# Two chained feed-forward nets after a retention layer: when the second net's weights are prepared, and which buffers their loads use

## The chip, the cores and the metric

The kernel runs on one core of a Trainium2 chip. The metric is the device time of one execution in microseconds (us). The core has five engines that work side by side, each through its own queue in the order of the program: TensorE (PE), VectorE (DVE), ScalarE (ACT), GpSimd (POOL), and SyncE (SP), which here only starts DMA transfers.

## What is computed

```python
def _moe_ref(x, w_in, w_out):
    h = x @ w_in
    g = np.where(h >= 1, h, np.where(h <= -1, 0.0, (h + 1) ** 2 / 4.0))
    return g @ w_out
def _moe2_ref(x, w1, w2, w3, w_out):
    a = x @ w1
    b = x @ w2
    h = a * b @ w3
    return h @ w_out
```

`x` are the 3072 tokens by 512 features that a retention layer (a decayed linear attention of 4 batches and 8 heads) gives. The first net has 2048 hidden features, the second 1024. The second net has nothing nonlinear behind its product `a * b`, so `w3 @ w_out` is computed once, and one product with it (`wc`) follows `a * b`.

## The kernel before, in words

Every fp32 operand is split into a rounded part and a rest (`split`, L96: a copy on ACT, then a subtraction on DVE), and three matmuls make one product (`mm3`, L100).

**First net.** The tokens are six tiles of 512, the hidden features 16 blocks of 128. A step `n` is one block of one tile (the loop at L774). On PE it is twelve matmuls of `emit_h(n + 1)` (the next step's first product) and twelve of `emit_y1(n)`. Between them stand, on ACT and DVE, the nonlinear function of the step to come (`emit_g1`, L456: `r`), its split (`emit_g2`, L466: `gh`, `gl`), and the split of a block of `w_out` (`emit_wo`, L476: `wo_s`). So `emit_y1` of the next step needs what ACT and DVE do behind `emit_h` of this one. `f = n - 80` counts the steps of the last tile, 0 to 15. The order on every queue is the order of the program; no scheduler changes it.

**Preparation in the last tile** (L840 to L852). `prepare_ab(j)` (L606) takes one block of `w1` and `w2` from DRAM (`fetch_ab`, two loads of 256 KB), makes four sums on DVE and seven splits on ACT and DVE, and writes the result back to DRAM with two transfers, `wab_d<-four` of 1 MB and `wab_d<-three` of 0.75 MB (L625). All eight preparations lie here, one in each odd step. Even steps load a block of the second `w_out` (`fetch(("wo2", j))`) and split the one before it (`load_wo2`, L552). All these loads go through `fetch` (L271), into one set of five buffers, and are issued on SP at L273, behind whatever SP has to issue before.

**The product of the last two weights** (L859 to L882). For `u` from 0 to 15, `emit_w3o(u)` (L563) is twelve matmuls with a block of `w3` and a block `wo2`; `load_w3(u + 1)` (two buffers) splits the next block, and the block after that is fetched. `evac_w3o` splits the four sums into `wc` at `u` = 7 and 15. In the same loop the first net's result for the first pair of tiles is read back (`fetch_y1`, four loads a half), added up (`add_y`, L641: four operations on DVE) and split (`split_y`, L654), seven splits a half, for the second net.

**Second net** (L885 on): `emit_ab(i, f, fill)` and `emit_out`; its weights come by `load_unit`, two loads of 1 MB and 0.75 MB. `c5` (L683) has one buffer of its own.

Of the kernel before, what the change touches and what calls it, by code (L numbers as in the profile page):

```python
# [9 lines left out]
F32 = mybir.dt.float32  # L10
# [6 lines left out]
P = 128  # L17
# [5 lines left out]
TT = 512  # L23
NTILE = NT // TT
NK = DM // P
NP = H // 2
NF1, NF2 = FF1 // P, FF2 // P
# [10 lines left out]
PLAIN = 11  # L38
SINGLE = 1
LATE = 5  # L40

# [5 lines left out]
def retention_then_two_ffns(  # L49
# [219 lines left out]
    arrived = {}  # L269

    def fetch(key, src):  # L271
        t = late.tile([P, 512], F32, tag="f", name="f32", bufs=5)
        nc.sync.dma_start(out=t, in_=src)  # L273
        arrived[key] = t

# [276 lines left out]
    def load_wo2(j):  # L552
        t = new_w("wo2")
        split(t[:, 0, :], t[:, 1, :], arrived.pop(("wo2", j)))
        wo2[j] = t
# [46 lines left out]
    def fetch_ab(f):  # L602
        for w in range(2):
            fetch(("wab", 2 * f + w), spill[("wab", 2 * f + w)])
# [31 lines left out]
    def fetch_y1(i, kb, which):  # L636

        for j in which:
            fetch(("y", i, kb, j), y1_d[2 * i + j % 2][kb + 2 * (j // 2)])
# [19 lines left out]
    def emit_ab(i, f, fill):  # L659
        w = units.pop(8 * i + f)  # L660
        bank = ps_h.tile([P, TT], F32, tag="h", name="bank_a")
        ps_p2 = ps_b.tile([P, TT], F32, tag="p2", name="bank_c")
        ps_p5 = ps_b.tile([P, TT], F32, tag="p5", name="bank_b")
        fill = list(fill)

        def product(name, ps, first):
            for kb in range(2):
                t, y = w[name], yops[(i, kb, name)]
                lh, ll, rh, rl = t[:, 0, kb, :], t[:, 1, kb, :], y[:, 0, :], y[:, 1, :]
                for k, (x, z) in enumerate(((lh, rh), (ll, rh), (lh, rl))):  # L670
                    nc.tensor.matmul(  # L671
                        out=ps, lhsT=x, rhs=z, start=first and kb + k == 0,
                        stop=kb == 1 and k == 2, skip_group_check=True,
                    )

        def between():
            if fill:
                emit_out(*fill.pop(0))

        c1 = work.tile([P, TT], F32, tag="r", name="c1")  # L680
        c2 = late.tile([P, TT], F32, tag="c2", name="c2", bufs=2)
        c3 = late.tile([P, TT], F32, tag="c3", name="c3", bufs=1)
        c5 = late.tile([P, TT], F32, tag="c5", name="c5", bufs=1)  # L683
        product("p1", bank, True)
        nc.scalar.copy(out=c1, in_=bank)
        product("p2", ps_p2, True)
        nc.vector.tensor_tensor(out=c1, in0=ps_p2, in1=c1, op=ALU.add)
        between()
        product("p6", bank, False)
        nc.scalar.copy(out=c2, in_=bank)  # L690
        product("p5", ps_p5, True)
        nc.scalar.copy(out=c5, in_=ps_p5)
        between()
        product("p7", bank, False)
        nc.scalar.copy(out=c3, in_=bank)
        product("p3", ps_p5, False)
        nc.vector.tensor_tensor(out=c2, in0=ps_p5, in1=c2, op=ALU.add)  # L697
        nc.vector.tensor_tensor(out=c3, in0=c3, in1=c5, op=ALU.add)
        nc.vector.tensor_tensor(out=c2, in0=c2, in1=c3, op=ALU.mult)
        between()  # L700
        product("p4", bank, False)
        nc.vector.tensor_tensor(out=c1, in0=bank, in1=c1, op=ALU.mult)
        between()
        ph = split_pool.tile([P, TT], F32R, tag="gh", name="ph")
        pl = split_pool.tile([P, TT], F32R, tag="gl", name="pl")
        split(ph, pl, c1)
        p0[f] = (ph, pl)
        ph = wpool.tile([P, TT], F32R, tag="wo", name="qh")
        pl = wpool.tile([P, TT], F32R, tag="wo", name="ql")
        split(ph, pl, c2)  # L710
        p1[f] = (ph, pl)
# [21 lines left out]
    with tc.manual_schedule():  # L733
# [40 lines left out]
        for n in range(-1, NA):  # L774
            last = n + 1 == NA
            if n < HALF - 1:
                mine = 1 if n % 2 else 2
            elif n < NF1 + 3:
                mine = 0
            elif n < NF1 + HALF - 2:  # L780
                mine = 1
            elif n < 2 * NF1 - 1:
                mine = (len(todo) - (NSTEP - 3 * TILE_PIECES) + 2 * NF1 - 2 - n) // (2 * NF1 - 1 - n)
            else:
                mine = 1 if (n + 1) % 4 < 3 else 0
            mine = [todo.popleft() for _ in range(mine) if todo]
            if n == PLAIN - 1:
                drain_conv()
                conversion.close()
                split_pool = splits.enter_context(tc.tile_pool(name="split_pool", bufs=2))  # L790
                cpool = conversion.enter_context(tc.tile_pool(name="cpool1", bufs=2))
                jobs.extend(later)
                load_job(jobs[0])
                load_job(jobs[1])
                for j in range(NF2):
                    jobs.append((w_out2[j], 512, ("wo2", j), done_spill(("wo2", j))))
                for j in range(NF2):
                    for i, w in enumerate((w1, w2)):
                        key = ("wab", 2 * j + i)
                        jobs.append((w[j], 512, key, done_spill(key)))  # L800
                for u in range(2 * NF2):
                    hf, j = divmod(u, NF2)
                    key = ("w3", u)
                    jobs.append((w3t[j][:, hf * 512:(hf + 1) * 512], 512, key, done_spill(key)))
            for i in range(2):
                if n == NF1 + (i + 1) * HALF - 4:
                    fetch_part(i)
            if n == NA - NF1:
                assert not todo
                drain_conv()  # L810
            f = n - (NA - NF1)
            if not last:
                emit_h(n + 1)
            if mine:
                piece_mm(mine[0])
                chunk_ahead(mine[0])
            if not last:
                emit_g1(n + 1)
            if mine:
                piece_ew(mine[0])  # L820
            if not last and f:
                emit_g2(n + 1)
            if n >= 0:
                emit_y1(n)
                evac_y1(n)
            if not f:

                conversion.close()
                splits.close()
                retention.close()  # L830
                split_pool = ctx.enter_context(tc.tile_pool(name="split_late", bufs=2))
                late = ctx.enter_context(tc.tile_pool(name="late", bufs=1))
                emit_g2(n + 1)
            if not last:
                emit_wo(n + 1)
            for a in mine[1:]:
                piece_mm(a)
                chunk_ahead(a)
                piece_ew(a)
            if f >= 0:  # L840
                j = f // 2
                if f % 2 == 0:
                    if j == 0:
                        fetch_ab(0)
                    else:
                        load_wo2(j - 1)
                    fetch(("wo2", j), spill[("wo2", j)])
                else:
                    prepare_ab(j)
                    if j + 1 < NF2:  # L850
                        fetch_ab(j + 1)
        load_wo2(NF2 - 1)  # L852
        pairs_psum.close()
        ps_b = ctx.enter_context(tc.tile_pool(name="ps_b", bufs=1, space=bass.MemoryType.PSUM))

        def y_of(i, kb):
            return [(i, kb, name) for name in ORDER]

        fetch(("w3", 0), spill[("w3", 0)])  # L859
        load_w3(0)  # L860
        fetch(("w3", 1), spill[("w3", 1)])
        fetch_y1(0, 0, range(4))
        for u in range(2 * NF2):
            load_w3(u + 1)
            if u + 2 < 2 * NF2:
                fetch(("w3", u + 2), spill[("w3", u + 2)])
            emit_w3o(u)
            hf, j = divmod(u, NF2)
            if j == NF2 - 1:
                evac_w3o(hf)  # L870
            if u == 0:
                add_y(0, 0)
            if u == NF2:
                add_y(0, 1)
            if u < NK + 3:
                split_y(*y_of(0, 0)[u])
                if u >= 3:
                    fetch_y1(0, 1, [u - 3])
            elif u > NF2:
                split_y(*y_of(0, 1)[u - NF2 - 1])  # L880
            if u in (2 * NF2 - 4, 2 * NF2 - 2):
                load_unit((u - 2 * NF2 + 4) // 2)  # L882


        for i in range(NTILE // 2):  # L885
            more = i + 1 < NTILE // 2
            ahead = y_of(i + 1, 0) + y_of(i + 1, 1)
            for f in range(NF2):
                emit_ab(i, f, out_blocks(f - 1) if 0 < f < NF2 - 1 else ())
                if 8 * i + f + 2 < 8 * (NTILE // 2):  # L890
# [95 lines left out]
```

## Time and profile before

| | us |
|---|---|
| median of three runs | 1108.55 (1107.0 to 1108.69) |
| the profiled execution's own time | 1108.74 |
| its span in the trace | 1106.9 |
| PE busy in the span | 1053.5 |
| DVE busy | 700.9 |
| ACT busy | 435.0 |

The rows of the profile have this form: start in us from the span's beginning, duration, engine, line and operation, output<-inputs by the program's names, tile sizes, count; in brackets the idle time of the engine before it and what ended it. `SPq` is SP's queue; an SP row is the issue of a transfer, not the transfer. The modelled durations of matmuls overlap, so a matmul's price is read from the distance between two starts. Busy engines say little by themselves: a stage is as long as the wait that ends last in it.

### The profile page before, as it was taken

The numbers are of one execution on the slowest core, as the hardware profiler recorded it, in microseconds if no ns is written. First come the engines' busy times: TensorE is split into PE (matmuls) and PEld (weight loads), VectorE is DVE, ScalarE is ACT, GpSimd is POOL, SyncE is SP. The second block draws the span as 40 slices with busy tenths as digits, with TensorE's granted clock in tenths as the row PEclk, the third lists the DMA queues.
The fourth block names the chain that finished last, engine by engine and source line by source line (L and its number), as shares of the span: only waits on it lengthen the run. The fifth ranks groups of instructions, "written<-read, shape, count | busy, mean of one in ns | idle before, by whom it ended". The sixth has DMA issues, their size and how long they took to land.

```text
span 1106.9 us, 14137 instructions
## 1 busy us (share of the span) xinstructions
PE 1053.5 (95%) x5444; PEld 832.1 (75%) x5444; DVE 700.9 (63%) x1130; ACT 435.0 (39%) x763; POOL 61.8 (6%) x51
## 2 busy tenths in 40 slices
PE   5789999899999999999999995899999999999998
PEld 4555578677777777777788784778888888888887
DVE  4698888688878878877835775553455344623341
ACT  1223355344444445444435664343233223412220
POOL 2212000011110100000000000000000000000000
PEclk9999999999999999999999997899999999999999
DMA  6545224345543444354302667554554355523412
GB/s 216 172 144 175 91 96 161 106 155 179 168 155 126 152 153 151 125 166 149 115 2 104 235 217 276 166 200 168 178 177 143 125 171 180 190 102 136 162 38 76
DMA packets 64116, 166.03 MB, mean 150 GB/s; under 512 B 7600, under 2 KB 15920, under 8 KB 59312
## 3 DMA queue, kind: packets, MB, share of 16 engines
q1 hardware_dynamic: 64048, 165.12, 44.0%
q8 instruction: 43, 0.70, 0.2%
q14 instruction: 25, 0.20, 0.1%
HBM read 125.24 MB, written 39.85 MB: 149 GB/s over the span
## 4 chain that ended last, share of the span: by engine, by line
PE 80%; DVE 8%; DMA 6%; ACT 3%; SPq 2%; issue 1%; POOL 0%; DVEq 0%; POOLq 0%; ACTq 0%
PE bank_a L671 12%; PE hps L102 7%; PE hps L103 7%; PE hps L101 7%; PE y1acc L101 7%; PE bank_b L671 6%; PE y1acc L102 6%; PE y1acc L103 6%; PE oacc L716 4%; PE oacc L718 4%; PE oacc L717 4%; DMA f<-sp_wab 3%; PE bank_c L671 3%; PE pa L370 3%; PE pa L346 2%; PE y1acc L511 1%
## 5 line engine op out<-in xcount | busy, mean ns | idle before, releaser
L101 PE MATMUL hps<-xh,win 128*128 128x512 f32 x384 | 155.6, 405 | 6.8 <-ACT win L97 5.5
L102 PE MATMUL hps<-xh,win 128*128 128x512 f32 x384 | 153.0, 398 | 0.7 <-DVE win L98 0.7
L103 PE MATMUL hps<-xl,win 128*128 128x512 f32 x384 | 152.0, 396 | 0.2 <-DVE xl L415 0.2
L101 PE MATMUL y1acc<-gh,wo_s 128*128 128x512 f32 x340 | 139.6, 411 | 6.6 <-ACT wo_s L97 6.6
L671 PE MATMUL bank_a<-yop,unit 128*128 128x512 f32 x576 | 145.7, 389 | 0.0
L459 ACT ACTIVATE r<-hps 128x512 f32<-128x512 f32 x96 | 57.3, 597 | 215.2 <-PE hps L103 215.2
L102 PE MATMUL y1acc<-gh,wo_s 128*128 128x512 f32 x340 | 135.6, 399 | 0.9 <-DVE wo_s L98 0.9
L103 PE MATMUL y1acc<-gl,wo_s 128*128 128x512 f32 x340 | 134.2, 395 | 0.0
L461 DVE SCALAR_TENSOR_TENSOR r<-hps,r 128x512 f32<-128x512 f32 x96 | 66.4, 691 | 99.4 <-ACT r L460 98.8
L671 PEld LDWEIGHTS bank_a<-yop,unit 128*128 128x128 f32 x576 | 108.0, 188 | 22.5
L697 DVE TENSOR_TENSOR c<-bank_b,c 128x512 f32<-128x512 f32 x24 | 16.6, 692 | 131.5 <-PE bank_b L671 131.5
L101 PEld LDWEIGHTS hps<-xh,win 128*128 128x128 f32 x384 | 73.3, 191 | 26.0 <-ACT win L97 6.2
L102 PEld LDWEIGHTS hps<-xh,win 128*128 128x128 f32 x384 | 73.3, 191 | 18.9 <-issue 1.7
L103 PEld LDWEIGHTS hps<-xl,win 128*128 128x128 f32 x384 | 73.4, 191 | 16.8 <-DVE xl L415 0.9
L101 PEld LDWEIGHTS y1acc<-gh,wo_s 128*128 128x128 f32 x340 | 64.3, 189 | 25.9 <-ACT wo_s L97 7.8
L102 PEld LDWEIGHTS y1acc<-gh,wo_s 128*128 128x128 f32 x340 | 64.6, 190 | 16.1 <-DVE wo_s L98 3.8
L103 PEld LDWEIGHTS y1acc<-gl,wo_s 128*128 128x128 f32 x340 | 64.6, 190 | 14.5
L472 ACT CAST gh<-r 128x512 fp32r<-128x512 f32 x85 | 52.9, 622 | 53.0 <-DVE r L461 53.0
L671 PE MATMUL bank_b<-yop,unit 128*128 128x512 f32 x288 | 73.1, 389 | 0.0
L473 DVE TENSOR_TENSOR gl<-r,gh 128x512 fp32r<-128x512 f32 x85 | 60.8, 716 | 14.9 <-ACT gh L472 13.8
L671 PEld LDWEIGHTS bank_b<-yop,unit 128*128 128x128 f32 x288 | 54.1, 188 | 11.2
L460 ACT ACTIVATE r<-r 128x512 f32<-128x512 f32 x96 | 60.6, 632 | 3.1
(150 smaller groups left out, 1686.7 us busy)
## 6 DMA issues: line engine op xcount, KB each, us to landing
unit<-wab_d SPq DMA_DIRECT2D x24, 1024.0 KB, 4.8
unit<-wab_d SPq DMA_DIRECT2D x24, 768.0 KB, 4.2
raw<-in_w_in_dram SPq DMA_DIRECT2D x64, 128.0 KB, 3.0
raw<-in_w_dram SPq DMA_DIRECT2D x16, 512.0 KB, 3.9
raw<-in_w3t_dram SPq DMA_DIRECT2D x16, 512.0 KB, 3.9
wab_d<-four SPq DMA_DIRECT2D x8, 1024.0 KB, 3.9
raw<-in_w_out_dram SPq DMA_DIRECT2D x14, 512.0 KB, 3.6
q_t<-in_qT_dram SPq DMA_DIRECT2D x24, 256.0 KB, 4.2
```

Of the source, the lines that this page charges most:

```text
L101: nc.tensor.matmul(out=ps, lhsT=lh, rhs=rh, start=first, stop=False)
L102: nc.tensor.matmul(out=ps, lhsT=ll, rhs=rh, start=False, stop=False)
L103: nc.tensor.matmul(out=ps, lhsT=lh, rhs=rl, start=False, stop=last)
L459: nc.scalar.activation(out=r, in_=hps[n], func=AF.Relu, bias=0.5, scale=0.5)
L460: nc.scalar.activation(out=r, in_=r, func=AF.Square)
L461: nc.vector.scalar_tensor_tensor(out=r, in0=hps.pop(n), scalar=1.0, in1=r, op0=ALU.max, op1=ALU.min)
L472: nc.scalar.copy(out=gh, in_=gs[n])
L473: nc.vector.tensor_tensor(out=gl, in0=gs[n], in1=gh, op=ALU.subtract)
L671: nc.tensor.matmul(out=ps, lhsT=x, rhs=z, start=first and kb + k == 0, stop=kb == 1 and k == 2, skip_group_check=True,)
L716: nc.tensor.matmul(out=ps, lhsT=lh, rhs=wh, start=(f == 0), stop=False)
L717: nc.tensor.matmul(out=ps, lhsT=lh, rhs=wl, start=False, stop=False)
L718: nc.tensor.matmul(out=ps, lhsT=ll, rhs=wh, start=False, stop=(f == NF2 - 1))
```

## The change

Of the eight preparations only six stay in the last tile; `prepare_ab(6)` and `prepare_ab(7)` move into the product, behind `emit_w3o(0)` and `emit_w3o(3)`. A block of `w1` and `w2` is fetched in the even step ahead of its preparation. The blocks `wo2` are fetched and split in steps 7 to 15, one a step, each split one step after its fetch. The first two blocks of `w3` are fetched in the last step. `fetch_y1` moves to `u` = 3 and 7, the splits of the first half to `u` = 5 to 8, and `load_unit` comes one `u` earlier. `wo2` and `w3` share two buffers, `w1`, `w2` and the read-back of the first net four others; `c5` goes to the set of four that the results and sums use.

```diff
+EARLY_AB = 6
     def fetch(key, src):
-        t = late.tile([P, 512], F32, tag="f", name="f32", bufs=5)
+        one = key[0] in ("wo2", "w3")
+        t = late.tile([P, 512], F32, tag="f" if one else "y", name="f32", bufs=2 if one else 4)
...
-        c5 = late.tile([P, TT], F32, tag="c5", name="c5", bufs=1)
+        c5 = work.tile([P, TT], F32, tag="st", name="c5", bufs=4)
...
             if f >= 0:
-                j = f // 2
-                if f % 2 == 0:
-                    if j == 0:
-                        fetch_ab(0)
-                    else:
-                        load_wo2(j - 1)
-                    fetch(("wo2", j), spill[("wo2", j)])
-                else:
-                    prepare_ab(j)
-                    if j + 1 < NF2:
-                        fetch_ab(j + 1)
-        load_wo2(NF2 - 1)
+                if f % 2 and f < 2 * EARLY_AB:
+                    prepare_ab(f // 2)
+                elif f % 2 == 0 and f <= 2 * EARLY_AB:
+                    fetch_ab(f // 2)
+                j = f - NF2
+                if j >= 0:
+                    load_wo2(j)
+                if -1 <= j < NF2 - 1:
+                    fetch(("wo2", j + 1), spill[("wo2", j + 1)])
+                if last:
+                    fetch(("w3", 0), spill[("w3", 0)])
+                    fetch(("w3", 1), spill[("w3", 1)])
...
-        fetch(("w3", 0), spill[("w3", 0)])
+        ahead = y_of(0)
         load_w3(0)
-        fetch(("w3", 1), spill[("w3", 1)])
-        fetch_y1(0, 0, range(4))
         for u in range(2 * NF2):
             load_w3(u + 1)
             if u + 2 < 2 * NF2:
                 fetch(("w3", u + 2), spill[("w3", u + 2)])
             emit_w3o(u)
             hf, j = divmod(u, NF2)
             if j == NF2 - 1:
                 evac_w3o(hf)
             if u == 0:
+                prepare_ab(EARLY_AB)
+                fetch_ab(EARLY_AB + 1)
+            elif u == 3:
+                prepare_ab(EARLY_AB + 1)
+                fetch_y1(0, 0, range(4))
+            elif u == 5:
                 add_y(0, 0)
+            elif u == 7:
+                fetch_y1(0, 1, range(4))
+            if u == 5:
+                split_y(*ahead.pop(0))
+            elif u in (6, 7, NF2):
+                split_y(*ahead.pop(0))
+                split_y(*ahead.pop(0))
+            elif u > NF2:
+                split_y(*ahead.pop(0))
             if u == NF2:
                 add_y(0, 1)
-            if u < NK + 3:
-                split_y(*y_of(0, 0)[u])
-                if u >= 3:
-                    fetch_y1(0, 1, [u - 3])
-            elif u > NF2:
-                split_y(*y_of(0, 1)[u - NF2 - 1])
-            if u in (2 * NF2 - 4, 2 * NF2 - 2):
-                load_unit((u - 2 * NF2 + 4) // 2)
+            if u in (2 * NF2 - 5, 2 * NF2 - 3):
+                load_unit((u - 2 * NF2 + 5) // 2)
```

## Rows read from the trace of the kernel before

**Rows 1.** The page: busy us of each engine, share of the span, instructions.

```profile
PE 1053.5 (95%) x5444; PEld 832.1 (75%) x5444; DVE 700.9 (63%) x1130; ACT 435.0 (39%) x763; POOL 61.8 (6%) x51
```

**Rows 2.** PE's waits, 570 to 800 us: total, times, longest.

```profile
PE w3acc L101 <- ACT w3s L97: 13.8, 2, 13.2
PE y1acc L101 <- ACT wo_s L97: 2.5, 2, 2.1
```

**Rows 3.** Stretches: length, busy time by engine, PEclk, DMA share, GB/s.

```profile
676.50:680.30 3.80, 3.58 (x8) 2.54 (x9) 2.10 (x4) 0.93 (x3) 0.00 (x0) 0.55 0.96 296
...
694.60:700.70 6.10, 6.03 (x14) 4.44 (x15) 4.66 (x7) 1.46 (x4) 0.00 (x0) 0.50 0.66 208
```

**Rows 4.** Timeline of PE: single matmuls, and the second net's first group.

```profile
649.61 0.39 PE L102 MATMUL y1acc<-gh,wo_s 128*128 128x512 f32 x1
...
652.33 0.39 PE L102 MATMUL hps<-xh,win 128*128 128x512 f32 x1
...
676.56 0.65 PE L101 MATMUL y1acc<-gh,wo_s 128*128 128x512 f32 x1 [2.07 <-ACT wo_s L97]
677.37 0.79 PE L102 MATMUL y1acc<-gh,wo_s 128*128 128x512 f32 x1 [0.16 <-DVE wo_s L98]
...
681.06 0.39 PE L103 MATMUL y1acc<-gl,wo_s 128*128 128x512 f32 x1
694.67 0.79 PE L101 MATMUL w3acc<-wo,w3s 128*128 128x512 f32 x1 [13.23 <-ACT w3s L97]
...
742.76 1.52 PE L671 MATMUL bank_a<-yop,unit 128*128 128x512 f32 x6
```

**Rows 5.** Timeline of SP: issues of transfers.

```profile
606.59 0.32 SPq L625 DMA_DIRECT2D wab_d<-three  x1
...
641.28 0.32 SPq L625 DMA_DIRECT2D wab_d<-three  x1
...
680.52 1.90 SPq L543 DMA_DIRECT2D y_d<-y1st  x3
...
687.39 0.32 SPq L625 DMA_DIRECT2D wab_d<-three  x1
687.76 2.48 SPq L273 DMA_DIRECT2D f<-sp_w  x2
690.29 5.41 SPq L273 DMA_DIRECT2D f<-y_d  x4
```

**Rows 6.** Timeline of ACT.

```profile
620.80 0.61 ACT L97 CAST wo<-f 128x512 fp32r<-128x512 f32 x1
...
643.08 0.62 ACT L97 CAST wo<-f 128x512 fp32r<-128x512 f32 x1
...
647.85 0.71 ACT L97 CAST four<-f 128x256 fp32r<-128x256 f32 x2 [0.81 <-DMA f<-sp_wab]
```

**Rows 7.** Timeline of DVE.

```profile
615.08 0.42 DVE L617 TENSOR_TENSOR s<-f 128x256 f32<-128x256 f32 x1 [1.44 <-DMA f<-sp_wab]
...
621.02 0.68 DVE L98 TENSOR_TENSOR wo_s<-wo_f,wo_s 128x512 fp32r<-128x512 f32 x1
...
624.60 0.69 DVE L98 TENSOR_TENSOR wo_s<-wo_f,wo_s 128x512 fp32r<-128x512 f32 x1
...
648.47 0.43 DVE L617 TENSOR_TENSOR s<-f 128x256 f32<-128x256 f32 x1 [0.63 <-DMA f<-sp_wab]
...
651.96 0.42 DVE L98 TENSOR_TENSOR three<-f,three 128x256 fp32r<-128x256 f32 x1
...
698.05 0.69 DVE L649 TENSOR_TENSOR t__5867<-f,f 128x512 f32<-128x512 f32 x1 [1.27 <-DMA f<-y_d]
...
721.67 0.69 DVE L98 TENSOR_TENSOR w3s<-f,w3s 128x512 fp32r<-128x512 f32 x1 [0.65 <-ACT w3s L97]
```

**Rows 8.** Transfers issued from 590 to 760 us: count, size, median us to landing.

```profile
f<-sp_w SPq DMA_DIRECT2D x16, 256.0 KB, 2.7
...
unit<-wab_d SPq DMA_DIRECT2D x3, 768.0 KB, 7.0
```

More of the change, by code (lines that the diff above doesn't have):

```diff
@@ L840, in retention_then_two_ffns, with y_of @@
             if f >= 0:
-                j = f // 2
-                if f % 2 == 0:
-                    if j == 0:
-                        fetch_ab(0)
-                    else:
-                        load_wo2(j - 1)
-                    fetch(("wo2", j), spill[("wo2", j)])
-                else:
-                    prepare_ab(j)
-                    if j + 1 < NF2:
-                        fetch_ab(j + 1)
-        load_wo2(NF2 - 1)
+                if f % 2 and f < 2 * EARLY_AB:
[10 more added lines that the diff above has]
+                    fetch(("w3", 1), spill[("w3", 1)])
         pairs_psum.close()
         ps_b = ctx.enter_context(tc.tile_pool(name="ps_b", bufs=1, space=bass.MemoryType.PSUM))
-        def y_of(i, kb):
-            return [(i, kb, name) for name in ORDER]
-        fetch(("w3", 0), spill[("w3", 0)])
+        def y_of(i):
+            return [(i, kb, name) for kb in range(2) for name in ORDER]
+        ahead = y_of(0)
         load_w3(0)
-        fetch(("w3", 1), spill[("w3", 1)])
-        fetch_y1(0, 0, range(4))
         for u in range(2 * NF2):
@@ L871, in retention_then_two_ffns @@
             if u == 0:
-                add_y(0, 0)
+                prepare_ab(EARLY_AB)
[4 more added lines that the diff above has]
+            elif u == 5:
+                add_y(0, 0)
+            elif u == 7:
[7 more added lines that the diff above has]
+                split_y(*ahead.pop(0))
             if u == NF2:
                 add_y(0, 1)
-            if u < NK + 3:
-                split_y(*y_of(0, 0)[u])
-                if u >= 3:
-                    fetch_y1(0, 1, [u - 3])
-            elif u > NF2:
-                split_y(*y_of(0, 1)[u - NF2 - 1])
-            if u in (2 * NF2 - 4, 2 * NF2 - 2):
-                load_unit((u - 2 * NF2 + 4) // 2)
+            if u in (2 * NF2 - 5, 2 * NF2 - 3):
+                load_unit((u - 2 * NF2 + 5) // 2)
+        assert not ahead
         for i in range(NTILE // 2):
             more = i + 1 < NTILE // 2
-            ahead = y_of(i + 1, 0) + y_of(i + 1, 1)
+            ahead = y_of(i + 1)
             for f in range(NF2):
```

## The prediction

> **What bounds the kernel now.** I read the page's busy times first: PE works 1053.5 of 1106.9 us, DVE and ACT far less, POOL 61.8 [rows 1]. So only what makes PE stand matters. PE's waits around the change [rows 2] name two: 13.8 us for the first block of `w3`, 2.5 us for `wo_s`. The timeline of PE [rows 4] places them. Twelve matmuls take 652.33 - 649.61 = 2.72 us, 0.227 each. The first net's last matmul starts at 681.06, so it ends its turn at E = 681.29; the product starts at 694.67: 13.4 us of nothing. Before that, 2.07 us go at 676.56, in the last step. Each stop has a tail: from 676.50 to 680.30 the granted clock is 0.55, from 694.60 to 700.70 it is 0.50, the 1.2 GHz level [rows 3]. There 14 matmuls take 6.10 us instead of 3.2, so 2.9 us behind a long stop; behind the 2 us stop, 681.06 - 677.37 = 3.69 for ten matmuls instead of 2.27, so 1.4.
>
> Why the product waits: SP issues the last preparation's `three` at 687.39 and only then the first blocks of `w3` [rows 5]. What stands behind such a pair of writes can be read at the preparation in step 7. I call T the issue of `three`. T is 641.28 [rows 5]; the first read behind it reaches ACT at 647.85 [rows 6], T + 6.57, the second reaches DVE at 648.47 [rows 7], 0.62 later. The preparation itself runs on DVE from 648.47 to 652.38 and gives the next T: 3.9 us. In the quiet stretch the same 256 KB take 2.7 us [rows 8].
>
> **The change part by part.** Nothing is added to or taken from the arithmetic; instructions of DVE, ACT and SP move, and none of POOL.
>
> *wo2, one block a step.* Today a `wo2` block is split a whole pair of steps after its fetch, and its copy on ACT starts at 643.08, without a wait [rows 6]. After the change `wo2` 0 is fetched in step 7 right behind the writes of `prepare_ab(3)` and split in step 8. Its copy can start at T + 6.57 = 647.85, 4.8 us later. Behind it on ACT and DVE stands all that step 9 makes for PE. From such a copy (620.80) to the end of the next `wo_s` on DVE (624.60 + 0.69) are 4.49 us [rows 6, 7]. So `wo_s` ends at 652.34, where PE takes it at 649.61 today [rows 4]: PE stands 2.7 us. The copy could start up to 649.61 - 4.49 = 645.12, T + 3.8, for nothing. Then `prepare_ab(4)` begins 4.4 us after the copy and takes 3.9: the next T is 641.28 + 6.57 + 4.4 + 3.9 = 656.2, not 652.4, and the one after it 671.1. A pair of steps takes 14.9 us where PE needs 10.9. Behind the last T, `wo2` 4 lands at 677.7, `wo_s` for step 14 ends at 682.2, the next one, with only a split in between, 624.60 - 621.02 = 3.58 later [rows 7] at 685.7, and eleven more matmuls give E = 688.2: **+6.9**. Without any of these waits the last step would want `wo_s` at 675.65, and E would be 678.2, -3.1; a landing 1.3 later each time gives +10.8.
>
> I weigh here a rule that speaks for the change. The Trainium skill, "DMA: Bandwidth & Descriptors", section "Anatomy of one DMA — SWDGE (gpsimd) path", fits the time of a transfer (on the GpSimd path) as 2.0 us plus bytes over 436 GB/s; from that I estimate 2.6 us for 256 KB. With that the copy would start in time and this term would be -3.1 instead of +6.9. The rows at 647.85 and 648.47 speak against it for reads behind a pair. The Trainium skill, "DMA: Bandwidth & Descriptors", section "Queues, rings and completion order", says that descriptors are consumed in ring order on each engine; by that rule the reads wait for the writes, and the trace agrees (6.57 against 2.7 us).
>
> *The hole.* Step 15 has no writes of a preparation any more. SP issues the last `y_d` write 1.1 us after E (680.52 + 1.90) [rows 5], then `w3` 0. With 2.7 us [rows 8] it would land at E + 3.8; because the writes of `y_d` are still under way I take 3.3, E + 4.4; the 6.57 of a pair would give E + 7.7. With the copy of 0.6, PE starts at E + 5.1 (bounds 4.5 and 8.4), not E + 13.4: **-8.3** (-8.9 to -5.0).
>
> *The product.* Its 192 matmuls need 43.6 us; today it takes 742.76 - 694.67 = 48.1. Now the two preparations and their writes lie in it, while a block of `w3` is fetched only two products, 5.4 us, ahead. `w3` 1 needs the buffer of the last `wo2`, lands near E + 5.0 and is split by E + 6.4; `prepare_ab(6)` follows on DVE, T = E + 10.3. Behind its writes come two blocks of `w1`, `w2`, then `w3` 3 as third read: T + 6.57 + 2 x 0.62 = E + 18.1, split by E + 19.45. From E + 5.1 PE needs 37 matmuls, 8.4 us, to use it: 5.9 late, in which the slow clock after the hole is hidden. `w3` 4 is split at E + 20.1, then `prepare_ab(7)`, T = E + 24.0. Behind those writes come four loads of `fetch_y1`, and `w3` 6 is the fifth read. Today the sixth read behind such a pair (two of `w3`, four of `y_d`) is waited for until 698.05, T + 10.7 [rows 5, 7]; the fifth I put at 10.0: E + 34.0, split by 35.35, due 36 matmuls after E + 19.45: 7.7 late. A stop of 7 us lies between the two whose tails I know, 1.4 and 2.9: 2.2. At `u` = 8, two more splits (1.3) stand on DVE ahead of `w3` 9, which has 0.65 to spare (721.67) [rows 7]: 0.7. The fourth load of the second half needs the buffer that the split of `b22` at `u` = 8 frees; `add_y` waits for it, and the split of `w3` 10 stands behind `add_y` on DVE: 0.6 + 2.7 + three operations of 0.65 + 0.7 = 6.1 after the split of `w3` 9, due after 2.7: 3.4. Its tail: 1.4. The sum is 43.6 + 5.9 + 7.7 + 2.2 + 0.7 + 3.4 + 1.4 = 64.9: **+16.8**. If reads need 2.7 throughout, the first two go and a tail behind the hole returns: 51.3, +3.2.
>
> *Nothing* for the rest. `load_unit` one `u` earlier lands 7.0 us after its issue [rows 8], and `w3` 14 0.6 behind it, about 1 us before its use; without that cover, 0.5. `c5` among four buffers waits for a result written four allocations earlier, steps away against some 3 us; bound 0 to 1. Fewer splits in steps 2 to 6 free ACT and DVE behind `wo_s`, where no one waits: 0 to -1.
>
> Sum: 6.9 - 8.3 + 16.8 = **+15.4**. On the span 1106.9 that is 1122.3; with the 1.84 outside the span 1124.1; the execution lies 0.2 above the median, so **1124**.
>
> **The rivals.** *Faster: reads are not held behind the writes.* It decides at the first read: if it lands before T + 3.8 in the last tile, ACT and DVE are in time. Then E = 678.2, the product starts at 683.3 and takes 51.3: 734.6, 8.2 earlier, **1100.5**. For it: the median of 2.7 [rows 8]. Against it: 6.57 and 7.2 behind a pair [rows 5 to 7], and `w3` 0 itself in the hole. Chance 0.16. The Trainium skill's fit of 2.0 us plus bytes over 436 GB/s ("DMA: Bandwidth & Descriptors", "Anatomy of one DMA — SWDGE (gpsimd) path") would make this the likeliest case; no row behind a pair of writes agrees.
>
> *Only the product pays:* `wo2` lands in time or PE finds slack: 678.2 + 5.1 + 64.9 = 748.2, +5.4, **1114**. Against it the slack ends at T + 3.8. Chance 0.07.
>
> *Only the last tile pays, the gain is eaten before the product starts:* 688.2 + 5.1 + 51.3 = 744.6, +1.8, **1110.5**, so the change does not do what it is written to do. Chance 0.07, half of it no difference.
>
> *Heavier queue:* behind T = 606.59 the second read came at 615.08 [rows 5, 7], 8.5, not 7.2. With 1.3 more at each of five pairs, +6.5: **1130.5**. Chance 0.08.
>
> **How the numbers follow.** The forecast has 0.62, with 1117 to 1130 of its own: the hole's bounds, the tails, and half a microsecond a pair. The range 1109 to 1132 takes in all but the faster rival and the ends. Faster by over 0.2% (2.2 us, about what a measurement of this kernel can tell): the first rival and a little, 0.17. Within: 0.05. Slower: 0.78.
>
> **What would show it.** Right: ACT's copies of `wo2` in steps 8, 10 and 12 wait for DMA some 4 us; T repeats after 14.9 us; E lies near 688; the hole is about 5 us; PE stands ahead of products 3, 6 (the longest, 7 us) and 10 for `w3`. Wrong: a `wo2` copy within 3.8 us of T, T still each 11.1, `w3` 6 there within 4 us of its issue, or a hole as long as before.

## The result and the profile after

The changed kernel takes 1124.47 us (median of 4 runs, 1124.01 to 1125.17), the kernel before 1108.62 in the same comparison: ratio 1.0146, 95% interval 1.0128 to 1.0163. It is 1.5% slower; 1124 was forecast. The profiled span is 1122.2 us, 15.3 more than before, where the sum of the prediction said 15.4.

First the page of the changed kernel (busy us, share, instructions): the engines have the same work to do as in [rows 1]. PE's busy time is 8 us longer with as many instructions: there are more stops, and behind most of them matmuls run at the slow clock (rows below).

```profile
PE 1061.5 (95%) x5444; PEld 836.2 (75%) x5444; DVE 699.1 (62%) x1130; ACT 434.3 (39%) x763; POOL 64.1 (6%) x51
```

Then PE's waits from 570 to 820 us (total, times, longest). In [rows 2] one wait of 13.2 us did nearly all the harm; now the same total stands in four waits, and `wo_s` costs 7.1 instead of 2.5.

```profile
PE w3acc L102 <- ACT w3s L98: 13.9, 4, 4.7
PE y1acc L102 <- ACT wo_s L98: 7.1, 5, 2.2
PE y1acc L103 <- DVE wo_s L99: 1.6, 5, 0.3
PE w3acc L103 <- DVE w3s L99: 1.2, 3, 0.7
```

The timeline of PE, to be read beside [rows 4], places them: three stops in steps 10, 12 and 14, the hole, three stops in the product, ahead of products 3, 6 and 10, and the start of the second net. The second matmul of a product is the first that needs DVE's half of the split; those of products 3, 6, 9 and 10 are shown too.

```profile
651.37 0.50 PE L102 MATMUL y1acc<-gh,wo_s 128*128 128x512 f32 x1 [2.04 <-ACT wo_s L98]
...
667.02 0.49 PE L102 MATMUL y1acc<-gh,wo_s 128*128 128x512 f32 x1 [2.25 <-ACT wo_s L98]
...
681.89 0.49 PE L102 MATMUL y1acc<-gh,wo_s 128*128 128x512 f32 x1 [1.49 <-ACT wo_s L98]
...
689.41 0.39 PE L104 MATMUL y1acc<-gl,wo_s 128*128 128x512 f32 x1
694.25 0.80 PE L102 MATMUL w3acc<-wo,w3s 128*128 128x512 f32 x1 [4.45 <-ACT w3s L98]
...
708.31 0.49 PE L102 MATMUL w3acc<-wo,w3s 128*128 128x512 f32 x1 [2.83 <-ACT w3s L98]
709.04 0.50 PE L103 MATMUL w3acc<-wo,w3s 128*128 128x512 f32 x1 [0.23 <-DVE w3s L99]
...
723.54 0.62 PE L102 MATMUL w3acc<-wo,w3s 128*128 128x512 f32 x1 [4.67 <-ACT w3s L98]
724.27 0.80 PE L103 MATMUL w3acc<-wo,w3s 128*128 128x512 f32 x1
...
734.35 0.50 PE L103 MATMUL w3acc<-wo,w3s 128*128 128x512 f32 x1 [0.26 <-DVE w3s L99]
...
739.10 0.49 PE L102 MATMUL w3acc<-wo,w3s 128*128 128x512 f32 x1 [1.97 <-ACT w3s L98]
740.31 0.50 PE L103 MATMUL w3acc<-wo,w3s 128*128 128x512 f32 x1 [0.71 <-DVE w3s L99]
...
758.13 1.52 PE L673 MATMUL bank_a<-yop,unit 128*128 128x512 f32 x6
```

E, the end of the first net on PE, is 689.41 + 0.23 = 689.64, against 681.29: 8.35 later. The hole is 694.25 - 689.64 = 4.6 us instead of 13.4: 8.8 shorter. The product takes 758.13 - 694.25 = 63.9 instead of 48.1: 15.8 longer. 8.35 - 8.8 + 15.8 = 15.35, all that the kernel lost in the trace; the second net takes as long as before (364.1 us in both). The hole shrank to a third, and 24 us came back for its 8.8, in front of it and behind it.

What the waits in the last tile hang on is read on two engines. SP's timeline gives the issues (T is that of `three`, as in [rows 5]), ACT's the copies of `wo2` (L98, `wo<-f`):

```profile
641.08 0.32 SPq L627 DMA_DIRECT2D wab_d<-three  x1
641.45 1.24 SPq L275 DMA_DIRECT2D f<-sp_wo  x1
...
655.97 0.32 SPq L627 DMA_DIRECT2D wab_d<-three  x1
656.38 1.20 SPq L275 DMA_DIRECT2D f<-sp_wo  x1
...
671.62 0.32 SPq L627 DMA_DIRECT2D wab_d<-three  x1
...
713.47 0.32 SPq L627 DMA_DIRECT2D wab_d<-three  x1
713.84 3.92 SPq L275 DMA_DIRECT2D f<-y_d  x4
```

```profile
647.64 0.62 ACT L98 CAST wo<-f 128x512 fp32r<-128x512 f32 x1 [4.68 <-DMA f<-sp_wo]
...
663.29 0.62 ACT L98 CAST wo<-f 128x512 fp32r<-128x512 f32 x1 [4.92 <-DMA f<-sp_wo]
...
678.15 0.62 ACT L98 CAST wo<-f 128x512 fp32r<-128x512 f32 x1 [4.13 <-DMA f<-sp_wo]
...
722.88 0.62 ACT L98 CAST w3s<-f 128x512 fp32r<-128x512 f32 x1 [8.97 <-DMA f<-sp_w]
```

The copies start 6.56, 7.32 and 6.53 us after T; T repeats after 14.9 and 15.65 us where PE needs 10.9. `w3` 6, issued behind `prepare_ab(7)`'s writes and four loads of the first net's result, is on ACT at 722.88, T + 9.4.

The stretches of the changed kernel (columns as in [rows 3]). First two that run from a T to the copy that waits for a load behind it: the 16 DMA engines have hardly any idle time in them (share 1.00 and 0.98) and move 348 GB/s. Then the hole, and two of those after it in which the clock had fallen (0.53, near the 1.2 GHz level).

```profile
655.97:663.29 7.32, 7.32 (x34) 5.89 (x33) 2.52 (x4) 1.65 (x4) 0.00 (x0) 1.00 1.00 348
...
713.47:722.88 9.41, 5.40 (x24) 4.15 (x22) 0.69 (x1) 0.44 (x2) 0.00 (x0) 1.00 0.98 348
...
689.60:694.20 4.60, 0.20 (x1) 0.00 (x0) 0.94 (x2) 1.72 (x3) 0.00 (x0) 0.88 0.93 320
694.20:700.20 6.00, 5.96 (x14) 4.41 (x15) 5.17 (x13) 2.95 (x9) 0.00 (x0) 0.53 0.32 105
...
724.20:727.40 3.20, 3.13 (x8) 2.50 (x9) 3.17 (x7) 1.47 (x3) 0.00 (x0) 0.53 0.33 82
```

### The profile page after: what moved, and what is told of

Its sections match the earlier page's. It is cut to its first block, busy times and chain, and to the rows that moved or that the text cites. A ratio compares the mean times of both kernels' runs of the same rounds, so it can differ in the third digit from the quotient of the medians.

```text
span 1122.2 us, 14126 instructions
## 1 busy us (share of the span) xinstructions
PE 1061.5 (95%) x5444; PEld 836.2 (75%) x5444; DVE 699.1 (62%) x1130; ACT 434.3 (39%) x763; POOL 64.1 (6%) x51
## 4 chain that ended last, share of the span: by engine, by line
PE 77%; DVE 9%; DMA 6%; ACT 4%; SPq 2%; issue 1%; POOL 0%; DVEq 0%; ACTq 0%; POOLq 0%
PE bank_a L673 11%; PE y1acc L102 7%; PE hps L103 7%; PE hps L102 7%; PE hps L104 6%; PE y1acc L103 6%; PE y1acc L104 6%; PE bank_b L673 6%; PE oacc L718 4%; PE oacc L719 4%; PE oacc L720 4%; PE bank_c L673 3%; PE pa L372 3%; DMA f<-sp_wo 2%; PE pa L348 2%; DMA f<-sp_wab 2%
## 5 line engine op out<-in xcount | busy, mean ns | idle before, releaser
L102 PE MATMUL y1acc<-gh,wo_s 128*128 128x512 f32 x340 | 140.5, 413 | 11.4 <-ACT wo_s L98 11.4
L102 PEld LDWEIGHTS y1acc<-gh,wo_s 128*128 128x128 f32 x340 | 64.9, 191 | 32.1 <-ACT wo_s L98 13.9
L103 PEld LDWEIGHTS y1acc<-gh,wo_s 128*128 128x128 f32 x340 | 64.9, 191 | 17.2 <-DVE wo_s L99 4.8
L673 PEld LDWEIGHTS bank_b<-yop,unit 128*128 128x128 f32 x288 | 54.1, 188 | 11.2
L99 DVE TENSOR_TENSOR wo_s<-wo_f,wo_s 128x512 fp32r<-128x512 f32 x85 | 61.0, 718 | 1.9 <-ACT wo_s L98 1.9
```

The source lines that it names most:

```text
L99: nc.vector.tensor_tensor(out=lo, in0=src, in1=hi, op=ALU.subtract)
L102: nc.tensor.matmul(out=ps, lhsT=lh, rhs=rh, start=first, stop=False)
L103: nc.tensor.matmul(out=ps, lhsT=ll, rhs=rh, start=False, stop=False)
L673: nc.tensor.matmul(out=ps, lhsT=x, rhs=z, start=first and kb + k == 0, stop=kb == 1 and k == 2, skip_group_check=True,)
```

## The experiments

The theory: a load that is issued behind the two writes of a preparation comes 6.5 us or more later, and the change put `wo2` and `w3` behind them where PE's operands are made. The rivals: the amount or the place of work on DVE and ACT; too few buffers; and, within the theory, whether it is SP's queue or the DMA engines that make the load late.

### wo2 loaded as before

```diff
-                j = f - NF2
-                if j >= 0:
-                    load_wo2(j)
-                if -1 <= j < NF2 - 1:
-                    fetch(("wo2", j + 1), spill[("wo2", j + 1)])
+                if f % 2 == 0:
+                    j = f // 2
+                    if j:
+                        load_wo2(j - 1)
+                    fetch(("wo2", j), spill[("wo2", j)])
                 if last:
+                    load_wo2(NF2 - 1)
                     fetch(("w3", 0), spill[("w3", 0)])
```

> The changed kernel with one part undone: the blocks of wo2 are again fetched in even steps and split a pair of steps later; everything else stays. Theory (reads wait behind the two writes of a preparation on SP's queue, and wo2's split stands in front of PE's operands): ACT's copies of wo2 wait no more, T repeats after 11.1 us instead of 15, the last matmul of the first net ends near 678 instead of 689.6, the hole stays 4.6 to 5.1 and the product 64: 11 us less than the changed kernel, about 1113. Rival (the amount of work on DVE and ACT sets the pace, wherever its data come from): the same instructions run on the same engines, so 1122 to 1126. Rival (two buffers for wo2 and w3 are too few): two buffers stay, so no gain either.

Measured: 1113.4 us, 11.1 less than the changed kernel (ratio to before 1.0044, 1.0027 to 1.0061). E is 678.00 + 0.23 = 678.2, 11.4 earlier; the hole stays (4.6 us), and the product too (64.0). SP's issues of `three` are 11.1 us apart again, as its timeline shows; PE's rows give E and the hole:

```profile
641.07 0.32 SPq L627 DMA_DIRECT2D wab_d<-three  x1
...
652.17 0.32 SPq L627 DMA_DIRECT2D wab_d<-three  x1
...
663.29 0.32 SPq L627 DMA_DIRECT2D wab_d<-three  x1
```

```profile
678.00 0.39 PE L104 MATMUL y1acc<-gl,wo_s 128*128 128x512 f32 x1
682.84 0.79 PE L102 MATMUL w3acc<-wo,w3s 128*128 128x512 f32 x1 [4.45 <-ACT w3s L98]
```

The same splits on the same engines, in the same two buffers: neither the amount of work nor the number of buffers cost the 11 us. But this run also takes every second split out of steps 8 to 15, so it does not tell the place of the splits from the place of the loads; the next run does.

### wo2 issued ahead of the writes, split where the change splits it

```diff
             if f >= 0:
+                if -1 <= f - NF2 < NF2 - 1:
+                    fetch(("wo2", f - NF2 + 1), spill[("wo2", f - NF2 + 1)])
                 if f % 2 and f < 2 * EARLY_AB:
...
-                if -1 <= j < NF2 - 1:
-                    fetch(("wo2", j + 1), spill[("wo2", j + 1)])
```

> The changed kernel with one line moved: in steps 7 to 14 the fetch of the next wo2 block is issued ahead of the step's preparation and its writes, or of its other loads, not behind them; the block is split in the same step as in the changed kernel. Theory: ACT's copies of wo2 in steps 8, 10 and 12 find their block there, T repeats after 11.1 to 11.8 us, the last matmul of the first net ends near 679, and the time is 1112 to 1115. Rival (it is the place of the split among ACT's and DVE's work in steps 8 to 15 that makes PE late, not the landing): PE keeps its stops, 1121 to 1126.

Measured: 1114.84 us. PE's stops for `wo_s` shrink to 0.9 us at most, and E is 679.75. Moving the issue of a load by one place gives back 9.6 of the 11 us, so the place of the split is not it either. The issues of `three` are 11.9 and 12.6 us apart here, more than the 11.1 to 11.8 expected. One load more in front of `w1` and `w2` would be 0.62 of that, by the distance of two reads in [rows 6, 7]; the rest stays open.

### w3 issued ahead of the writes in the product

```diff
+    def two(u):
+        t = late.tile([P, 1024], F32, tag="wc", name="two", bufs=NF2)
+        pair[("w3", u)] = t[:, 0:512]
+        pair[("w3", u + 1)] = t[:, 512:1024]
...
-            if u + 2 < 2 * NF2:
-                fetch(("w3", u + 2), spill[("w3", u + 2)])
+            if u in (0, 3):
+                two(u + 3)
+            for w in {0: (2, 3, 4), 1: (), 2: (), 3: (5, 6, 7, 8), 4: (), 5: (), 6: ()}.get(u, (u + 2,)):
+                if w < 2 * NF2:
+                    fetch(("w3", w), spill[("w3", w)])
```

> The changed kernel with w3 blocks 3 and 4 issued ahead of the writes of prepare_ab(6), and 5 to 8 ahead of those of prepare_ab(7); four of them lie in two tiles of the set that wc uses later, so no buffer is waited for. Theory (queue behind the writes): PE's stops ahead of products 3 and 6 go, 13 us of stops and tails; but add_y(0, 0), at u = 5, now waits for the read-back of the first net, which still stands behind the writes, and the split of w3 block 7 stands behind add_y on DVE: a new stop of about 6 us ahead of product 7. In sum 5 to 8 us less, 1117 to 1120. Rival (the preparations' own 3.9 us on DVE make the stops): they stay where they are, so within 2 us of 1124.5.

Measured: 1120.88 us, 3.6 less, just outside what was expected. The stops ahead of products 3 and 6 are gone. The new one ahead of product 7 is there, as DVE's timeline and then PE's show:

```profile
718.84 0.69 DVE L659 TENSOR_TENSOR t__5950<-f,f 128x512 f32<-128x512 f32 x1 [5.89 <-DMA f<-y_d]
...
722.65 0.69 DVE L99 TENSOR_TENSOR w3s<-two,w3s 128x512 fp32r<-128x512 f32 x1
```

```profile
719.27 0.50 PE L102 MATMUL w3acc<-wo,w3s 128*128 128x512 f32 x1 [1.68 <-ACT w3s L98]
723.39 0.79 PE L103 MATMUL w3acc<-wo,w3s 128*128 128x512 f32 x1 [3.62 <-DVE w3s L99]
```

`add_y` waits 5.89 us for a load behind the writes, and the block of `w3` that lies ready stands behind it on DVE. A stop was exchanged for another that stands behind the same writes. The run also gives four blocks buffers of their own, but in the changed kernel it was not a buffer that held these loads back: DVE was through with `w3` 1, whose buffer `w3` 3 takes, at 695.8, and with `w3` 4, whose buffer `w3` 6 takes, at 709.6, both before the writes were issued (T = 699.67 and 713.47).

### The last stop of the product alone

```diff
                 fetch(("w3", u + 2), spill[("w3", u + 2)])
+            if u == NF2:
+                fetch_y1(0, 1, [3])
+            if u == NF2 + 1:
+                add_y(0, 1)
             emit_w3o(u)
...
-                fetch_y1(0, 1, range(4))
+                fetch_y1(0, 1, range(3))
```

(`add_y(0, 1)` no longer stands at `u` = 8.)

> The changed kernel with the last stop of the product treated alone: w3 block 10 is fetched ahead of the fourth load of the read-back, and add_y(0, 1) stands behind the split of block 10, one u later. Theory: the stop ahead of product 10 (3.1 us and a tail of 1.4) goes, a smaller one of some 1 us comes ahead of product 11, because the fourth load still waits for the split of b22: 2 to 4 us less, 1120.5 to 1122.5. Rival (DVE is full there, and add_y makes PE late wherever it stands): 1123.5 to 1125.5.

Measured: 1123.11 us, 1.4 less, between the two expectations and not enough to decide. The stop of 2 us ahead of product 10 and its tail are gone from the trace, but 1.0 us stays inside product 10 and 1.4 come at the start of product 13. In that trace the product by itself takes 61.5 us instead of 63.9, 2.4 less; the first net, which the edit does not touch, ended 1.0 later, and that hides a part of the gain.

### The writes on another queue

```diff
-            nc.sync.dma_start(out=d, in_=t[:, 0:len(names), :].bitcast(F32))
+            nc.gpsimd.dma_start(out=d, in_=t[:, 0:len(names), :].bitcast(F32))
```

> The changed kernel with all sixteen writes of the preparations issued on GpSimd's queue instead of SP's; bytes, order of the engines' work and buffers stay. It parts two forms of the theory. If it is the order in SP's queue that holds the reads, they land some 3 to 5 us after the writes' issue instead of 6.6, the waits of wo2 and w3 shrink by at least half, and the time falls to 1105 to 1115. If it is the bandwidth of the 16 DMA engines, which both queues share, the reads land as late as before and the time stays within 1121 to 1127.

Measured: 1108.91 us, 15.6 less than the changed kernel and within 0.1% of the one before (ratio 1.0003, 0.9994 to 1.0013). The number fits the first form, but the trace shows another reason. SP's row for `wo2` 0:

```profile
620.04 0.83 SPq L275 DMA_DIRECT2D f<-sp_wo  x1
```

SP no longer waits for DVE to finish a preparation before it issues the writes, so it runs ahead: this load, meant for step 7, goes out at 620, long before that step's writes (POOL issues them at 640.7 and 641.7). So the run did not tell order in the queue from lack of bandwidth. A load that happened to be issued close behind POOL's writes was late here too: `w3` 6, issued at 701.0 with the second write at 700.9, is on ACT at 708.5.

### The same, with SP held back

```diff
+        if one:
+            nc.vector.memset(t[:, 0:1], 0.0)
         nc.sync.dma_start(out=t, in_=src)
```

(on top of the run before)

> The kernel with the writes on GpSimd's queue, and one more thing: a 1-column memset on DVE stands ahead of each load of wo2 and w3, so that SP issues these loads no earlier than DVE is through with what stands before them, the preparation included. Two ingredients are parted: that SP issues the loads only when the preparation is done, and that on SP's own queue the loads then stand behind the writes. If the order in one queue holds them, they land 3 to 4 us after their issue though the writes run, the copies of wo2 come in time, and the time stays near the 1109 of the kernel with the writes on GpSimd's queue (1107 to 1113). If the 16 DMA engines are what is short, on whatever queue, they land some 6 us after T again and the time is back at 1119 to 1127.

Measured: 1132.32 us, even above the upper expectation of 1127. The three rows of `wo2` 2 are POOL's, SP's and ACT's:

```profile
652.99 0.53 POOL L629 DMA_DIRECT2D wab_d<-three  x1 [0.48 <-DVE three L99]
...
653.37 0.32 SPq L277 DMA_DIRECT2D f<-sp_wo  x1
...
659.97 0.62 ACT L98 CAST wo<-f 128x512 fp32r<-128x512 f32 x1 [4.83 <-DMA f<-sp_wo]
```

6.6 us from issue to use with the writes on POOL's queue; in the changed kernel, all on SP, the same block took 663.29 - 656.38 = 6.9. `wo2` 4 took 6.6 here too; `wo2` 0, issued 0.24 us ahead of `three` but behind `four`, took 4.7. So a load need not stand behind the writes in one queue to be late. What the two runs have in common is that it is issued when up to 1.75 MB of writes have just gone to the same 16 DMA engines. From POOL's issue to the copy these have no idle time, as in the changed kernel:

```profile
652.99:659.97 6.98, 5.95 (x25) 4.38 (x24) 2.27 (x5) 1.39 (x4) 0.53 (x1) 1.00 1.00 354
```

The Trainium skill, "DMA: Bandwidth & Descriptors", section "Issuing engines are not separate DMA queues", says that transfers run on the same 16 engines and interleave, whichever engine starts them. The trace agrees that they share them, 6.6 against 6.9 us; how two queues interleave, it does not show, nor whether it is the engines or the memory behind them that is full at some 350 GB/s.

The run overshoots because the hold also stands ahead of every other block of `w3`: the product has ten waits for `w3s` on ACT and lasts 766.50 - 692.45 = 74.0 us. For the product it is no clean test; for `wo2` it is.

### The kernel before, with the first blocks of w3 ahead of the last writes

```diff
                 else:
+                    if last:
+                        fetch(("w3", 0), spill[("w3", 0)])
+                        fetch(("w3", 1), spill[("w3", 1)])
                     prepare_ab(j)
```

(their issue behind the loop is taken out)

> The kernel before with one thing moved: the first two blocks of w3 are fetched ahead of the last preparation instead of behind its writes. Theory: the product starts when the preparation's splits are through ACT, near 687.3 instead of 694.7, but the read-back of the first net still stands behind the writes, add_y at u = 0 waits for it with DVE, and product 2 stops for some 3 to 4 us: 3 to 5 us faster than before, about 1104.5. Rival (the last preparation's work and the waits for its buffers make the hole, not the queue): within 2 us of before, 1107 to 1110.

Measured: 1107.09 us, ratio 0.998 (0.9971 to 0.999): faster by some 1.6 us, less than the 3 to 5 expected, and just inside the rival's range. The hole shrinks to 7.3 us, and the stop ahead of product 2 is there (1.2 and 1.4 us, for `w3` behind `add_y`). But the hole did not shrink to what was worked out: the last preparation waits for two buffers that `y_d`'s writes free, 3.0 us here (1.7 before), and `w3`'s split stands behind it. So both sides of that expectation hold a part: the queue, and the preparation's own place.

### No load that PE needs behind the writes

```diff
+        tag, bufs = ("f", 2) if key[0] == "wo2" else ("y", 4)
+        if key[:3] == ("y", 0, 0):
+            tag, bufs = ("c2", 2) if key[3] < 2 else ("f", 2)
...
+            if last:
+                load_w3(0)
             if n >= 0:
                 emit_y1(n)
...
+                elif f % 2 == 0:
                     fetch_ab(f // 2)
+                if f % 2 == 0:
+                    j = f // 2
+                    if j:
+                        load_wo2(j - 1)
+                    fetch(("wo2", j), spill[("wo2", j)])
+                    two(f)
+                    fetch(("w3", f), spill[("w3", f)])
+                    fetch(("w3", f + 1), spill[("w3", f + 1)])
+                if last:
+                    load_wo2(NF2 - 1)
+                    fetch_y1(0, 0, range(4))
...
+            for part in parts.get(u, ()):
+                next(part)
+            if u == 4:
+                fetch_y1(0, 1, range(4))
+            elif u == 5:
+                add_y(0, 0)
+            elif u == NF2 + 1:
+                add_y(0, 1)
+            for _ in range(splits_at.get(u, 0)):
+                split_y(*ahead.pop(0))
```

(`parts` runs `prepare_ab(6)` and `prepare_ab(7)` as generators: sums, `four`, `three` of the one at `u` = 0, 1, 2, of the other at 2, 3, 4.)

> A version of the changed kernel in which no load that PE waits for stands behind the writes of a preparation: wo2 as in the kernel before, all blocks of w3 and the two last blocks of w1 and w2 fetched during the last tile (w3 into the tiles that wc takes later), the read-back of the first half fetched in step 15 into buffers of c2 and wo2, the first split of w3 ahead of the last y1 product, the two preparations in three pieces over products 0 to 4, add_y at u = 5 and 9. Theory: the first net ends near 678, the hole is under 1 us, the product takes 44 to 47 us, and the second net starts near 723 to 726 instead of 742.8: 1088 to 1092. Rival (DVE, with 40 us of work in a product of 44, becomes the bound): 1096 to 1104. Rival (4 MB more to load in the last tile delay the preparations): the first net ends later than 681 and the time is 1092 to 1100.

Measured: 1089.4 us, ratio to before 0.9827 (0.9811 to 0.9844): 19 us faster than the kernel before, 35 faster than the changed one. PE has no wait for `w3` left; these are all of its waits from 570 to 820 us:

```profile
PE y1acc L102 <- ACT wo_s L98: 1.3, 2, 0.8
PE y1acc L103 <- DVE wo_s L99: 0.6, 2, 0.3
```

On its timeline the product follows the first net without a hole, and the second net starts at 723.46:

```profile
679.35 0.39 PE L104 MATMUL y1acc<-gl,wo_s 128*128 128x512 f32 x1
679.58 0.39 PE L102 MATMUL w3acc<-wo,w3s 128*128 128x512 f32 x1
...
723.46 1.52 PE L689 MATMUL bank_a<-yop,unit 128*128 128x512 f32 x6
```

723.46 - 679.58 = 43.9 us for 192 matmuls, the pace of 0.227 almost without a loss. Both rivals of this run fall: DVE carries its work in that time, and the extra loads in the last tile delay little: E is 679.6, within 2 us of the 678 expected and not above 681, and T repeats after 11.2 us. The run moves many things at once, so it shows what they are worth together, not one by one.

## Why the prediction was right, step by step

*wo2 in the last tile: +6.9 forecast, +8.35 measured.* The three copies waited, the period of T was 14.9 us as worked out, then 15.65, because one block came 7.3 instead of 6.57 us behind its T. With that, DVE has the last `wo_s` ready at 686.2, from which E would be 688.7: 0.5 of the missing 1.45. The other 0.9 is the tail: the stop of 1.49 us at 681.89 brought the slow clock for eight matmuls in step 14, some 1.7 us; the rest of it does not show, since step 15 would have waited for its `wo_s` anyway. I had given no tail to the stops in the loop. Moving wo2 alone (two runs) gave back 11.4 and 9.9 us of E, so the cause is shown.

*The hole: -8.3 forecast, -8.8 measured.* PE started at E + 4.6, where the sum had E + 5.1 with a lower bound of 4.5.

*The product: +16.8 forecast, +15.8 measured.* Product 3's second matmul started at 709.04, E + 19.4 (forecast 19.45). Since PE had started half a microsecond earlier, that is 6.4 late and not 5.9. `w3` 6 came at T + 9.4 instead of the 10.0 that I put for a fifth load: product 6's second matmul, at 724.27, is 15.23 us behind that of product 3 where PE needs 8.17, so 7.1 late instead of 7.7. The tail behind it is 1.5, forecast 2.2. Product 9 cost 0.5 (0.7), product 10 3.1 and a tail of 1.7 (3.4 and 1.4). With 43.6 for the matmuls these make the measured 63.9, against 64.9. The terms mis-sized most are the fifth load and its tail, 0.6 and 0.7, both on the high side. That the whole sum comes out within 0.1 us is luck: the last tile was 1.45 too low, the hole 0.5 and the product 1.0 too high. Not forecast, too: the stop ahead of product 3 has a tail of 1.7 us, which costs nothing by itself, since the next stop ends with a load. That the loads behind the writes make the first two stops is shown by the run that issues `w3` ahead of them; the third was reduced, not removed, by the run on it alone (the product 2.4 us shorter, where it and its tail are worth 4.8), so its mechanism is only partly shown.

*What was forecast at nothing* (`load_unit` earlier, `c5` in the shared set, fewer splits in the early steps) shows no wait of PE in the trace, and the second net takes 364.1 us before and after. None was tried by itself.

*The rivals.* "Reads are not held" falls with the rows at 647.64, 663.29 and 678.15: 6.5 to 7.3 us, not 2.7. One reason given in the prediction is not borne out, though: it let the order of the descriptors in a queue explain why loads are held, and said the trace agrees. 6.57 us is what the trace shows, but the run with the writes on another queue, and SP held back, shows 6.6 from issue to use as well. What both have is the 16 engines without idle time; for the changed kernel, where all goes through SP, the two reasons give the same sum, since it rests on the measured 6.57 and on neither of them.

## What to carry to other kernels

When work that ends in large writes is moved next to a short stage, look at what is loaded behind those writes, and who waits for it in order: here a load of 256 KB behind 1.75 MB could be used 6.5 us or more after the second write's issue, in a stage that looked 5.4 us ahead. For `wo2`, moving only the issue of the loads ahead of the writes gave back 9.6 us; in the product the same gave 3.6, because other loads still stood behind the writes. Another queue helped here only because SP was then not held back. Buffers that a later stage owns (here `wc` and `c2`) can hold early loads without more memory.

## What was not expected

Putting the writes on GpSimd's queue gave all of the 15.6 us back, and not through the queue: SP, no longer waiting for DVE, issued loads far earlier (`wo2` 0 at 620 instead of 641). And a stop of only 1.5 us was followed by the slow clock (682.69 to 686.18 at 0.43 us a matmul, granted clock 0.60 from 682.0 to 686.2), as was one of 2.04 us at 651.37, while one of 2.25 us at 667.02 was not (1.00 from 667.0 to 670.0): the length of the stop alone does not tell.
